# Two-layer MLP behind retention and a Fourier mix: the half-sums of weights and tokens at other program steps

## The chip, the cores and the metric

One core of one Trainium2 chip runs the whole kernel in one launch. The metric is the device time of one execution in microseconds, the median over runs. TensorE is PE in the profile, VectorE DVE, ScalarE ACT, GpSimd POOL, SyncE SP.

## The reference

Everything is float32, with B=2, S=768 tokens, 512 features, and a hidden width of 2048. The MLP weights come as float64.

```python
def _moe_ref(x, w_ch1, w_ch2):            # x: the retention layer's output
    X = np.fft.fft(np.fft.fft(x, axis=1), axis=2)
    u = x + np.real(X)
    un = (u - mean(u)) / np.sqrt(var(u) + 1e-06)
    return u + np.maximum(un @ w_ch1, 0.0) @ w_ch2

def _moe2_ref(x, g_ln, w_ch1, w_ch2):
    xn = (x - mean(x)) / np.sqrt(var(x) + 1e-06) * g_ln
    return x + np.maximum(xn @ w_ch1, 0.0) @ w_ch2
```

Ahead of them stands a retention layer (block-wise attention with decay, 8 heads of 64).

## The kernel before, in words

Every float32 operand of a matmul is split into a high and a low float16 half, and three products (high-high, high-low, low-high) are added up. The program runs batch 0's retention and Fourier mix in an order written out by hand, and then a main loop (L1020) over program steps n = 0 to 127 and three more. Step n stands for layer m = n // 64, token block blk (16 steps each; a block is 384 tokens, two for each batch) and hidden tile f = n % 16. Steps 0 to 63 are layer one (m = 0), steps 32 to 47 its block 2, the first block of batch 1.

At a step stand, in this order: the up-projection of the step's tile (`mlp_up`, L655, with its matmuls in L662, or `mlp_up_fast`, L733, matmuls in L752), the background tasks that `put` (L939) entered for the step, and the down-projection `mlp_down` of the tile three steps back (matmuls in L799). Batch 1's retention and Fourier mix, the normalisation of later blocks and the conversion of weights are such background tasks. A scheduler places the instructions of each engine from this program order; each engine runs its own in that order, so a late instruction holds all behind it on the same engine.

The plain up-projection of a tile is 12 matmuls of 384 columns. The fast one computes two tiles together by a seven-product scheme (as Strassen's), on 192 columns. Its operands are sums of quarters: for the weights, `w1_sums(m, g, kk)` (L682) for group g of four tiles (f = 4g to 4g+3) and half kk of the features; for the tokens, `un_sums(m, blk, kk)` (L710). One call of `w1_sums`, a **unit** in the text below, issues on DVE two sums of a high and a low half (L695) and four sums of quarters (L700 to L703), then two casts on ACT (L706) and two subtractions on POOL (L707). One call of `un_sums` issues two L715 and L720 to L723 on DVE, two casts on ACT (L727) and two subtractions on POOL (L728). The first product of a pair needs no sum; the second needs both halves kk of weights and tokens.

In layer one the fast form is used from tile 4 of block 2 on (`F02` = 4, in `fast_from`, L1006): groups 1, 2 and 3 are first used at steps 36, 40 and 44, group 0 at step 48, in block 3. The sums of block 1's tokens are made and not used.

Each plain tile leaves PE through one `mlp_act` (L674): ACT writes the high half (L676), DVE the low half (L677), and only then is its PSUM bank, one of two in the pool "up", free for the tile two steps on. In the fast form ACT copies the first product (L764), DVE adds (L765, L772, L773, L778, L779), and PE writes over the same banks in between, so that PE waits for L765 and L772 within a pair; ACT and DVE take the result out in L784 and L785.

The steps of the units before: group 2 at 15 and 16, group 3 at 19 and 20, group 0 at 28 and 29, group 1 at 32 and 33. Block 1's token sums stand at 17 and 18, block 2's at 34 and 35. The normalisation of block 2 (three tiles of 128 tokens, `ln_a`, `ln_n`, `ln_b`) stands at the end of the Fourier mix of batch 1, just ahead of step 32, and its last act is a pair of transposing transfers on SP (L627) into `unT`, from which block 2's first matmul reads.

Where the sums lie: `i` in L684 numbers the units, and picks a room for each: two tiles of the loading pool "ld" (i < 3), the rooms of the mask and of three tables that are no longer needed (i = 3 to 6), or the two state tiles (i = 7).

Of the kernel before, what the change touches and what calls it, by code (L numbers as in the profile page):

```python
# [49 lines left out]
ONPOOL = "Y1 Y2 o0 o1 k0 k1 k2 j0 j1 j2"  # L50
LD1 = ()
LD2 = ()
EARLY0, GATEN, B1, SPC, DS, DC, DFO, DD, D1S, D2S, AO, YA, NR, NE, LN1, L1, L2, F01, F02, S2, S0, SD, TL, R1, R2, SE, PR0, PR1, LAG, UB, FB, NW, MQ, SPL = 11, 8, 3, 2.0, 2.0, 5, 1.0, 0.5, 0.5, 1.0, "aba", "aa", 2, 0, 2, 2.5, 2.5, 16, 4, 15, 28, 1, 3, 1.5, 2, "dddd_dppp", 0, 0, 3, 3, 13, 11, 1, 3

KEEP = -(1 << 30)
REST = (1 << 30) - 1
# [57 lines left out]
def tile_retention_fourier_mlp(ctx: ExitStack, tc: tile.TileContext, a: dict, out: bass.AP):  # L114
# [23 lines left out]
    def f32t(name, spare=None):  # L138
        if spare is not None:
            return wpool.tile([P, 512], F32, tag=f"w2_{spare}", name=name)  # L140
        return fp.tile([P, 512], F32, tag="f", name=name)

    def hl(name):
        return fp.tile([P, 2, 512], F16, tag="f", name=name)
# [536 lines left out]

    def w1_sums(m, g, kk, r=None):  # L682
        w = w1t[m, g]
        i = (2 * g + kk - 4) % 8  # L684
        if 3 <= i < 7:
            t = const.tile([P, 2, 2, 2, 256], F16, tag=f"big{i - 3}", name=f"sw{m}_{g}_{kk}")
            t = [t[:, 0], t[:, 1]]
        elif i < 3:
            t = [ldp.tile([P, 2, 2, 256], F16, tag="ld", name=f"sw{m}_{g}_{kk}_{x}") for x in range(2)]
        else:  # L690
            t = [const.tile([P, 2, 2, 256], F16, tag=f"state{x}", name=f"sw{m}_{g}_{kk}_{x}") for x in range(2)]
        if r is None:
            r = [f32t(f"wr{m}_{g}_{k}") for k in (kk, kk + 2)]
            for x, k in enumerate((kk, kk + 2)):
                dve.tensor_tensor(r[x], w[:, 0, k], w[:, 1, k], op=ALU.add)  # L695
        eng = [pool if z == "p" else dve for z in SE.split("_")[m]]
        (a11, a21), (a12, a22) = ([z.rearrange("p (q a f) -> p q a f", a=2, f=P)[:, :, x] for x in range(2)] for z in r)
        s12, s34 = (f32t(f"ws{x}_{m}_{g}_{kk}") for x in (12, 34))
        s1, s2, s3, s4 = (z[:, x * 256:x * 256 + 256].rearrange("p (q f) -> p q f", f=P) for z in (s12, s34) for x in range(2))
        eng[0].tensor_tensor(s1, a21, a22, op=ALU.add)  # L700
        eng[1].tensor_tensor(s2, s1, a11, op=ALU.subtract)
        eng[2].tensor_tensor(s3, a11, a21, op=ALU.subtract)
        eng[3].tensor_tensor(s4, a12, s2, op=ALU.subtract)  # L703
        for x, z in enumerate((s12, s34)):
            hi, lo = (t[x][:, y].rearrange("p s f -> p (s f)") for y in range(2))
            act.copy(hi, z)  # L706
            pool.tensor_tensor(lo, z, hi, op=ALU.subtract)  # L707
        sw[m, g, kk] = t

    def un_sums(m, blk, kk):  # L710
        x = unT[m, blk]
        r = []
        for k in (kk, kk + 2):
            t = f32t(f"tr{m}_{blk}_{k}")[:, :TB]
            dve.tensor_tensor(t, x[:, 0, k], x[:, 1, k], op=ALU.add)  # L715
            r += [t[:, :HB], t[:, HB:]]
        b11, b12, b21, b22 = r
        t12, t34 = (f32t(f"ts{y}_{m}_{blk}_{kk}")[:, :TB] for y in (12, 34))
        t1, t2, t3, t4 = t12[:, :HB], t12[:, HB:], t34[:, :HB], t34[:, HB:]
        dve.tensor_tensor(t1, b12, b11, op=ALU.subtract)  # L720
        dve.tensor_tensor(t2, b22, t1, op=ALU.subtract)
        dve.tensor_tensor(t3, b22, b12, op=ALU.subtract)
        dve.tensor_tensor(t4, b21, t2, op=ALU.subtract)  # L723
        tw[m, blk, kk] = []
        for y, z in enumerate((t12, t34)):
            t = hl(f"th{y}_{m}_{blk}_{kk}")[:, :, :TB]
            act.copy(t[:, 0], z)  # L727
            pool.tensor_tensor(t[:, 1], z, t[:, 0], op=ALU.subtract)  # L728
            tw[m, blk, kk].append(t)
# [209 lines left out]
    def put(n, task):  # L939
        bg.setdefault(max(int(n), 0), []).append((n, len(bg), task))  # L940

    def later(task, offset):
        def run():
            with tc.high_priority(offset=-offset):
                task()
        return run
# [14 lines left out]
    n = t + DC + DFO  # L961
# [28 lines left out]
    def w1_unit(p):  # L990
        g, kk, half = p // 4, p % 4 // 2, p % 2
        t = w_conv(1, 1, 4 * g + kk + 2 * half)
        if not half:
            first[g, kk] = t
        else:
            w1_sums(1, g, kk, (first.pop((g, kk)), t))
# [5 lines left out]
    def step(n):  # L1002
        m = n // (NB * NF)
        return m, order[m][n // NF % NB], n % NF
# [3 lines left out]
    for (m, blk), f in fast_from.items():  # L1008
        for kk in range(2):
            if m == 0 and blk < 3:  # L1010
                put(16 * blk + f / 2 + kk - (7 if blk == 1 else 0), lambda blk=blk, kk=kk: un_sums(0, blk, kk))
            else:
                at = m * NB * NF + order[m].index(blk) * NF
                put(at - TL + 2 * kk, lambda m=m, blk=blk, kk=kk: un_sums(m, blk, kk))
    for g in range(4):
        for kk in range(2):
            n = (S2 if g > 1 else S0) + 4 * (g % 2) + SD * kk
            put(n, later(lambda g=g, kk=kk: w1_sums(0, g, kk), PR0))

    for n in range(total + LAG):  # L1020
        rest = None
        if n < total:
            m, blk, f = step(n)
# [34 lines left out]
```

## Time and profile before

| what | value |
|---|---|
| time, median of 3 runs | 645.83 us (644.15 to 646.98) |
| the profiled execution's own time | 646.34 us |
| its span, first to last instruction | 644.5 us |
| mean granted clock of TensorE | 0.968 of 2.4 GHz |
| PE busy | 587.3 us, 91% |
| DVE busy | 470.2 us, 73% |
| POOL busy | 296.0 us, 46% |
| ACT busy | 259.4 us, 40% |

Times in the views are microseconds from the start of the span, the mean of one instruction in nanoseconds. "xN" counts instructions, and a bracket at a row's end gives the idle time of the engine just ahead of it and what ended it. Matmuls are pipelined, so the duration of a row of N matmuls is less than N times that of one.

### The profile page before, as it was taken

The page shows a single profiled execution, that of the slowest core. Times are in us where ns is not written, and L with a number is a line of the kernel's source. Part 1 is how long each engine was busy: PE and PEld are TensorE (multiplying, and loading weights), DVE is VectorE, ACT ScalarE, POOL GpSimd, SP SyncE. Part 2 cuts the span into 40 slices and gives each one's busy share as a digit, 9 for nine tenths or more (in the row PEclk, how much of TensorE's full clock was granted, in tenths as well). Part 3 has the DMA queues.
Part 4 walks back from the last instruction along what each step waited for, and adds up shares of the span by engine and source line. Part 5 has one row for each costly group of instructions (what it writes and reads, how often), then busy time and mean ns, then how long its engine had stood idle before and what let it go on. Part 6 is the DMA issues. An engine that isn't in the chain of part 4 may idle for free.

```text
span 644.5 us, 11965 instructions
## 1 busy us (share of the span) xinstructions
PE 587.3 (91%) x4704; PEld 384.2 (60%) x4704; DVE 470.2 (73%) x985; ACT 259.4 (40%) x524; POOL 296.0 (46%) x303
## 2 busy tenths in 40 slices
PE   6868878979998999859999988799999999999997
PEld 4743734545554454437676755576677676777773
DVE  5999798998599945965569999999663653454333
ACT  3634557764433332233226754575323222321111
POOL 6865767876536456372116886598211210120000
PEclk8879988999999999989999998999999999999999
DMA  8971017975200001001115664384020015201001
GB/s 286 395 295 48 20 67 194 258 245 177 91 1 1 1 9 33 9 16 26 10 34 146 181 147 129 102 204 108 1 67 17 17 54 55 41 2 70 30 1 50
DMA packets 44020, 58.66 MB, mean 91 GB/s; under 512 B 25919, under 2 KB 27836, under 8 KB 43964
## 3 DMA queue, kind: packets, MB, share of 16 engines
q1 hardware_dynamic: 43292, 57.82, 30.9%
q8 instruction: 37, 0.61, 0.4%
q10 hardware_dynamic: 672, 0.08, 0.1%
q14 instruction: 19, 0.16, 0.1%
HBM read 49.23 MB, written 4.72 MB: 84 GB/s over the span
## 4 chain that ended last, share of the span: by engine, by line
PE 59%; DVE 27%; issue 5%; POOL 4%; ACT 3%; DMA 2%; DVEq 0%; ACTq 0%; SPq 0%; POOLq 0%
PE ps_y L799 28%; PE ps L752 21%; PE ps_h L662 4%; DVE wf L259 3%; DVE ps_w L255 3%; DVE ps_w L257 2%; DVE bst L596 2%; DMA ws<-in_w 2%; DVE tr L715 1%; POOL m L320 1%; DVE h L677 1%; PE ps_s L308 1%; PE ps_d L484 1%; DVE wr L695 1%; POOL w L272 1%
## 5 line engine op out<-in xcount | busy, mean ns | idle before, releaser
L799 PE MATMUL ps_y<-w,h 128*128 128x512 f16 x1152 | 280.5, 381 | 4.6 <-ACT h L784 2.2
L799 PEld LDWEIGHTS <-h 128*128 128x128 f16 x1152 | 109.6, 98 | 108.3 <-ACT h L784 5.0
L752 PEld LDWEIGHTS <-sw 128*128 128x128 f16 x1104 | 96.9, 100 | 25.9 <-issue 11.7
L752 PE MATMUL ps<-th,sw 128*128 128x192 f16 x828 | 94.8, 252 | 9.5 <-ACT th L727 7.4
L272 POOL TENSOR_TENSOR w<-wf,w 128x512 f16<-128x512 f32 x64 | 75.3, 1182 | 53.9 <-ACT w L270 53.7
L752 PEld LDWEIGHTS <-w 128*128 128x128 f16 x828 | 72.0, 98 | 22.5 <-issue 6.3
L662 PE MATMUL ps_h<-unT,w 128*128 128x384 f16 x396 | 75.9, 335 | 9.2 <-DVE h L677 5.1
L784 ACT ACTIVATE h<-ps 128x384 f16<-128x384 f32 x92 | 43.4, 488 | 68.4 <-DVE ps L778 58.6
L752 PE MATMUL ps<-unT,w 128*128 128x192 f16 x552 | 62.5, 247 | 3.1 <-DVE h L677 3.1
L662 PEld LDWEIGHTS <-w 128*128 128x128 f16 x396 | 38.1, 100 | 41.2 <-issue 10.6
L728 POOL TENSOR_TENSOR th<-ts,th 128x384 f16<-128x384 f32 x28 | 25.4, 924 | 65.2 <-ACT th L727 65.1
L772 DVE TENSOR_TENSOR t<-ps,s 128x192 f32<-128x192 f32 x46 | 16.3, 354 | 53.3 <-PE ps L752 53.3
L785 DVE SCALAR_TENSOR_TENSOR h<-ps,h 128x384 f16<-128x384 f32 x92 | 48.8, 552 | 5.8 <-ACT h L784 4.5
L707 POOL TENSOR_TENSOR sw<-ws,sw 128x512 f16<-128x512 f32 x32 | 40.4, 1276 | 21.5 <-ACT sw L706 21.5
L764 ACT COPY s<-ps 128x192 f32<-128x192 f32 x46 | 14.6, 317 | 82.4 <-PE ps L752 82.3
L269 ACT ACTIVATE wf<-wf 128x512 f32<-128x512 f32 x48 | 30.1, 629 | 37.2 <-DVE wf L259 37.1
L625 POOL TENSOR_TENSOR uns<-un,uns 128x512 f16<-128x512 f32 x21 | 25.1, 1195 | 41.7 <-ACT uns L624 41.7
L255 DVE TENSOR_SCALAR ps_w<-ws 128x512 int32<-128x512 int32 x54 | 37.0, 687 | 3.7 <-DMA ws<-in_w 3.0
L270 ACT CAST w<-wf 128x512 f16<-128x512 f32 x64 | 39.2, 615 | 1.2
L765 DVE TENSOR_TENSOR s<-ps,s 128x192 f32<-128x192 f32 x46 | 16.2, 352 | 30.6 <-ACT s L764 30.6
L604 POOL TENSOR_TENSOR rs<-rs,neghalf 128x1 f32<-128x1 f32 x24 | 13.6, 573 | 53.3 <-DVE rs L602 52.9
L259 DVE SCALAR_TENSOR_TENSOR wf<-ws,ps_w 128x512 int32<-128x512 int32 x54 | 36.6, 678 | 1.1
(153 smaller groups left out, 880.9 us busy)
## 6 DMA issues: line engine op xcount, KB each, us to landing
ws<-in_w SPq DMA_DIRECT2D x25, 512.0 KB, 4.7
ws<-in_w2b SPq DMA_DIRECT2D x16, 512.0 KB, 3.3
ws<-in_w1b SPq DMA_DIRECT2D x16, 512.0 KB, 4.0
kt<-in_kt SPq DMA_DIRECT2D x12, 256.0 KB, 5.4
qt<-in_qt SPq DMA_DIRECT2D x12, 256.0 KB, 5.4
v<-in_v SPq DMA_DIRECT2D x12, 256.0 KB
k<-in_k SPq DMA_DIRECT2D x12, 256.0 KB, 3.3
pre<-in_w SPq DMA_DIRECT2D x4, 512.0 KB, 6.6
```

The lines of the kernel that those rows point to most:

```text
L255: dve.tensor_scalar(part, raw[:, :, 1], 3, REST, op0=ALU.logical_shift_left, op1=ALU.bitwise_and)
L259: dve.scalar_tensor_tensor(ti, raw[:, :, 0], 29, part, op0=ALU.logical_shift_right, op1=ALU.bitwise_or)
L269: act.activation(t, t, AF.Copy, scale=sc)
L270: act.copy(hi, t)
L272: (dve if m == 0 and i in (LD1 if kind == 1 else LD2) else pool).tensor_tensor(lo, t, hi, op=ALU.subtract)
L662: pe.matmul(ps, w[:, i, k, fo:fo + P], x[:, j, k, :], start=n == 0, stop=n == 11)
L707: pool.tensor_tensor(lo, z, hi, op=ALU.subtract)
L728: pool.tensor_tensor(t[:, 1], z, t[:, 0], op=ALU.subtract)
L752: pe.matmul(ps, lhs, rhs, start=start and n == 0, stop=n == 5, skip_group_check=True)
L784: act.activation(hi, z, AF.Relu)
L785: dve.scalar_tensor_tensor(lo, z, 0.0, hi, op0=ALU.max, op1=ALU.subtract)
L799: pe.matmul(dn[blk][j], h[:, x, j * P:(j + 1) * P], w[:, y], start=f == 0 and n == 0, stop=f == NF - 1 and n == 2)
```

## The change

The units of layer one get a table of steps, in the order in which the groups are used: group 1 at 16 and 18, group 2 at 20 and 25, group 3 at 28 and 30, group 0 at 36 and 40. Block 2's token sums go from steps 34 and 35 to 31 and 32; block 1's stay. The number i of a unit's room becomes 2g + kk - 2 modulo 8, so that the first three units in the new order take the "ld" tiles; this holds for layer two as well, whose units stay at their steps. `later(..., PR0)` with PR0 = 0 falls away.

```diff
-EARLY0, GATEN, ... F01, F02, S2, S0, SD, TL, R1, R2, SE, PR0, PR1, LAG, ... = 11, 8, ... 16, 4, 15, 28, 1, 3, 1.5, 2, "dddd_dppp", 0, 0, 3, ...
+EARLY0, GATEN, ... F01, F02, TL, R1, R2, SE, PR1, LAG, ... = 11, 8, ... 16, 4, 3, 1.5, 2, "dddd_dppp", 0, 3, ...
+
+SUMS = {(1, 0): 16, (1, 1): 18, (2, 0): 20, (2, 1): 25, (3, 0): 28, (3, 1): 30, (0, 0): 36, (0, 1): 40}
...
-        i = (2 * g + kk - 4) % 8
+        i = (2 * g + kk - 2) % 8
...
-                put(16 * blk + f / 2 + kk - (7 if blk == 1 else 0), lambda blk=blk, kk=kk: un_sums(0, blk, kk))
+                put(16 * blk + f / 2 + kk - (7, 3)[blk - 1], lambda blk=blk, kk=kk: un_sums(0, blk, kk))
...
-    for g in range(4):
-        for kk in range(2):
-            n = (S2 if g > 1 else S0) + 4 * (g % 2) + SD * kk
-            put(n, later(lambda g=g, kk=kk: w1_sums(0, g, kk), PR0))
+    for (g, kk), n in SUMS.items():
+        put(n, lambda g=g, kk=kk: w1_sums(0, g, kk))
```

No instruction is added or taken away on any engine (PE 8906 rows, DVE 974, ACT 523, POOL 305, SP 161 in both). From line 56 to the last edit the changed file's line numbers are two higher. In the rows below, `wr_g_k` and `ws_0_g_kk` are the weight sums of group g, `sw_g_kk` their halves, `tr`, `ts` and `th` the same for tokens, `h_b_p` pair p of hidden tiles of block b, `ps_h_b_f` the up-projection of tile f, and `u`, `un`, `uns` the normalisation.

**Place 1: the end of block 1, ACT.** First before, then with the change: `h_1_7<-ps_h_1_15` is the last hidden tile of block 1, `un_2_2` the last tile of tokens of block 2's normalisation.

```order
L534 ACTIVATE qs_189<-ps_pq_2_3037 128x128
L534 ACTIVATE qs_189<-ps_pq_2_3037 128x127
L676 ACTIVATE h_1_7_3254<-ps_h_1_14_3241 128x384
L676 ACTIVATE h_1_7_3254<-ps_h_1_15_3266 128x384
L616 ACTIVATE un_2_2_3089<-u_120,rs_2_2_3062 128x512
L624 CAST uns_2_2_3092<-un_2_2_3089 128x512
L571 ACTIVATE cosy_2_3099<-ps_pq_2_3037 128x129
```

```order
L536 ACTIVATE qs_189<-ps_pq_2_3022 128x128
L536 ACTIVATE qs_189<-ps_pq_2_3022 128x127
L678 ACTIVATE h_1_7_3239<-ps_h_1_14_3226 128x384
L708 CAST sw_2_1_3074<-ws_0_2_1_3079 128x512
L708 CAST sw_2_1_3074<-ws_0_2_1_3080 128x512
L678 ACTIVATE h_1_7_3239<-ps_h_1_15_3266 128x384
L618 ACTIVATE un_2_2_3089<-u_120,rs_2_2_3047 128x512
L626 CAST uns_2_2_3092<-un_2_2_3089 128x512
L573 ACTIVATE cosy_2_3099<-ps_pq_2_3022 128x129
```

The two casts of group 2's second unit now stand ahead of the last hidden tile. On DVE the unit's six sums stand in the same place, around `u<-u,qs` and ahead of `u<-ps_pq_2`, on which the normalisation goes on; before and with the change:

```order
L615 SCALAR_TENSOR_TENSOR rs_2_1_2994<-mv_2_1_2992,rs_2_1_2994 128x1
L539 TENSOR_TENSOR u_120<-u_120,qs_189 128x257
L677 SCALAR_TENSOR_TENSOR h_1_7_3254<-ps_h_1_14_3241,h_1_7_3254 128x384
L677 SCALAR_TENSOR_TENSOR h_1_7_3254<-ps_h_1_15_3266,h_1_7_3254 128x384
L549 SCALAR_TENSOR_TENSOR u_120<-ps_pq_2_3037,u_120 128x256 x2
```

```order
L617 SCALAR_TENSOR_TENSOR rs_2_1_2979<-mv_2_1_2977,rs_2_1_2979 128x1
L697 TENSOR_TENSOR wr_2_1_3075<-w_0_2_1396 128x512
L697 TENSOR_TENSOR wr_2_3_3076<-w_0_2_1396 128x512
L541 TENSOR_TENSOR u_120<-u_120,qs_189 128x257
L702 TENSOR_TENSOR ws_0_2_1_3079<-wr_2_1_3075,wr_2_3_3076 128x256
L704 TENSOR_TENSOR ws_0_2_1_3080<-wr_2_1_3075 128x256
L679 SCALAR_TENSOR_TENSOR h_1_7_3239<-ps_h_1_14_3226,h_1_7_3239 128x384
L703 TENSOR_TENSOR ws_0_2_1_3079<-ws_0_2_1_3079,wr_2_1_3075 128x256
L705 TENSOR_TENSOR ws_0_2_1_3080<-wr_2_3_3076,ws_0_2_1_3079 128x256
L679 SCALAR_TENSOR_TENSOR h_1_7_3239<-ps_h_1_15_3266,h_1_7_3239 128x384
L551 SCALAR_TENSOR_TENSOR u_120<-ps_pq_2_3022,u_120 128x256 x2
```

Two sums went ahead of the row with `qs`, four behind it, on both sides of the hidden tile `h_1_7<-ps_h_1_14`.

**Place 2: the first steps of block 2, DVE**, up to the release of the banks of hidden tiles 2 and 3 (`h_2_1`); before and with the change:

```order
L702 TENSOR_TENSOR ws_0_1_1_3352<-wr_1_1_3347 128x256
L715 TENSOR_TENSOR tr_2_0_3393<-unT_2_2945 128x384
L715 TENSOR_TENSOR tr_2_2_3395<-unT_2_2945 128x384
L615 SCALAR_TENSOR_TENSOR rs_3_2_3665<-mv_3_2_3663,rs_3_2_3665 128x1
L677 SCALAR_TENSOR_TENSOR h_2_1_3383<-ps_h_2_2_3370,h_2_1_3383 128x384
L703 TENSOR_TENSOR ws_0_1_0_3312<-wr_1_2_3308,ws_0_1_0_3311 128x256
L701 TENSOR_TENSOR ws_0_1_1_3351<-ws_0_1_1_3351,wr_1_1_3347 128x256
L720 TENSOR_TENSOR ts_0_2_0_3397<-tr_2_0_3393 128x192
L722 TENSOR_TENSOR ts_0_2_0_3398<-tr_2_2_3395,tr_2_0_3393 128x192
L599 BN_AGGR mv_0_2_4531<-bst_0_2_4529 128x2
L703 TENSOR_TENSOR ws_0_1_1_3352<-wr_1_3_3348,ws_0_1_1_3351 128x256
L677 SCALAR_TENSOR_TENSOR h_2_1_3383<-ps_h_2_3_3421,h_2_1_3383 128x384
```

```order
L705 TENSOR_TENSOR ws_0_3_1_3248<-wr_3_3_3244,ws_0_3_1_3247 128x256
L723 TENSOR_TENSOR ts_0_2_0_3285<-tr_2_2_3283,ts_0_2_0_3285 128x192
L617 SCALAR_TENSOR_TENSOR rs_3_2_3649<-mv_3_2_3647,rs_3_2_3649 128x1
L679 SCALAR_TENSOR_TENSOR h_2_1_3384<-ps_h_2_2_3371,h_2_1_3384 128x384
L725 TENSOR_TENSOR ts_0_2_0_3286<-tr_2_2_3283,ts_0_2_0_3285 128x192
L601 BN_AGGR mv_0_2_4532<-bst_0_2_4530 128x2
L717 TENSOR_TENSOR tr_2_1_3322<-unT_2_2930 128x384
L717 TENSOR_TENSOR tr_2_3_3324<-unT_2_2930 128x384
L598 BN_STATS bst_1_2_5473<-u_119 128x6
L722 TENSOR_TENSOR ts_0_2_1_3326<-tr_2_1_3322 128x192
L724 TENSOR_TENSOR ts_0_2_1_3327<-tr_2_3_3324,tr_2_1_3322 128x192
L679 SCALAR_TENSOR_TENSOR h_2_1_3384<-ps_h_2_3_3406,h_2_1_3384 128x384
```

Four weight sums (`ws`) in these rows have become one, and the second half of the token sums (`tr_2_1`, `tr_2_3`) is begun ahead of tile 3's row rather than behind it.

**Place 3: the first fast pair of block 2, DVE** (`s_2_4`, `t_2_5`); before and with the change:

```order
L615 SCALAR_TENSOR_TENSOR rs_0_0_4181<-mv_0_0_4179,rs_0_0_4181 128x1
L599 BN_AGGR mv_1_0_5121<-bst_1_0_5119 128x2
L765 TENSOR_TENSOR s_2_4_3473<-ps_2_4_3474,s_2_4_3473 128x192
L772 TENSOR_TENSOR t_2_5_3517<-ps_2_4_3474,s_2_4_3473 128x192
L765 TENSOR_TENSOR s_2_6_3555<-ps_2_6_3556,s_2_6_3555 128x192
L773 TENSOR_TENSOR ps_2_4_3475<-ps_2_4_3475,t_2_5_3517 128x192
L602 TENSOR_SCALAR rs_0_1_4339<-mv_0_1_4337 128x1
L778 TENSOR_TENSOR ps_2_4_3474<-ps_2_4_3474,s_2_4_3473 128x192
```

```order
L601 BN_AGGR mv_1_0_5123<-bst_1_0_5121 128x2
L697 TENSOR_TENSOR wr_0_0_3466<-w_0_0_742 128x512
L697 TENSOR_TENSOR wr_0_2_3467<-w_0_0_742 128x512
L767 TENSOR_TENSOR s_2_4_3442<-ps_2_4_3443,s_2_4_3442 128x192
L702 TENSOR_TENSOR ws_0_0_0_3470<-wr_0_0_3466,wr_0_2_3467 128x256
L704 TENSOR_TENSOR ws_0_0_0_3471<-wr_0_0_3466 128x256
L703 TENSOR_TENSOR ws_0_0_0_3470<-ws_0_0_0_3470,wr_0_0_3466 128x256
L705 TENSOR_TENSOR ws_0_0_0_3471<-wr_0_2_3467,ws_0_0_0_3470 128x256
L774 TENSOR_TENSOR t_2_5_3501<-ps_2_4_3443,s_2_4_3442 128x192
L775 TENSOR_TENSOR ps_2_4_3444<-ps_2_4_3444,t_2_5_3501 128x192
L767 TENSOR_TENSOR s_2_6_3539<-ps_2_6_3540,s_2_6_3539 128x192
L780 TENSOR_TENSOR ps_2_4_3443<-ps_2_4_3443,s_2_4_3442 128x192
```

Group 0's first unit now stands around the row of `s_2_4`, four of its sums ahead of `t_2_5`; its second unit stands in the same way around `s_2_8`.

## Rows read from the trace of the kernel before

**Rows 1.** Busy time of each engine by stretch (core 0), then granted clock and DMA.
```profile
254.00:286.00 32.00, 20.97 (x116) 10.73 (x114) 30.17 (x60) 10.47 (x22) 19.10 (x17) 0.97 0.07 13
286.00:310.00 24.00, 23.25 (x183) 17.70 (x183) 11.57 (x31) 7.24 (x16) 5.13 (x6) 0.89 0.19 29
```
**Rows 2.** Waits of PE from 195 to 310 us: total, times, longest.
```profile
PE ps L752 <- ACT th L727: 4.9, 1, 4.9
PE ps L752 <- DVE h L677: 3.1, 2, 2.1
PE ps_h L662 <- DVE h L677: 2.6, 1, 2.6
PE ps_d L484 <- ACT fhl L474: 2.3, 2, 1.7
PE ps L752 <- DVE t L772: 0.4, 1, 0.4
PE ps_h L662 <- DMA unT<-uns: 0.4, 1, 0.4
PE ps L752 <- DVE s L765: 0.2, 1, 0.2
```
**Rows 3.** PE in order of time, 245 to 296 us: start, duration, instruction.
```profile
249.31 7.72 PE L799 MATMUL ps_y<-w,h 128*128 128x512 f16 x35
...
286.08 4.16 PE L752 MATMUL ps<-th,sw 128*128 128x192 f16 x25 [4.95 <-ACT th L727]
290.40 1.00 PE L752 MATMUL ps<-th,sw 128*128 128x192 f16 x6 [0.16 <-DVE s L765]
...
292.84 0.66 PE L752 MATMUL ps<-th,sw 128*128 128x192 f16 x6
293.33 0.66 PE L752 MATMUL ps<-unT,w 128*128 128x192 f16 x6
```
**Rows 4.** Busy time by stretch, as Rows 1, five microseconds.
```profile
285.00:290.00 5.00, 3.92 (x25) 3.72 (x25) 1.11 (x6) 1.32 (x4) 1.79 (x3) 0.50 0.15 30
```
**Rows 5.** DVE by line, 254 to 286 us: count, busy us, mean ns.
```profile
L695 DVE TENSOR_TENSOR wr<-w 128x512 f32<-128x512 f16 x8 | 6.6, 866 | 0.0
...
L703 DVE TENSOR_TENSOR ws<-wr,ws 128x256 f32<-128x256 f32 x4 | 3.1, 771 | 0.0
L701 DVE TENSOR_TENSOR ws<-ws,wr 128x256 f32<-128x256 f32 x4 | 2.3, 581 | 0.0
L702 DVE TENSOR_TENSOR ws<-wr 128x256 f32<-128x256 f32 x4 | 2.2, 544 | 0.0
...
L715 DVE TENSOR_TENSOR tr<-unT 128x384 f32<-128x384 f16 x4 | 2.1, 568 | 0.0
...
L700 DVE TENSOR_TENSOR ws<-wr,wr 128x256 f32<-128x256 f32 x4 | 1.8, 441 | 0.0
```
**Rows 6.** DVE in order of time, 179 to 256 us.
```profile
180.01 2.88 DVE L695 TENSOR_TENSOR wr<-w 128x512 f32<-128x512 f16 x2
...
245.43 0.80 DVE L539 TENSOR_TENSOR u<-u,qs 128x257 f32<-128x257 f32 x1 [2.22 <-ACT qs L534]
...
249.16 0.56 DVE L677 SCALAR_TENSOR_TENSOR h<-ps_h,h 128x384 f16<-128x384 f32 x1 [2.47 <-ACT h L676]
...
254.34 1.28 DVE L695 TENSOR_TENSOR wr<-w 128x512 f32<-128x512 f16 x2
```
**Rows 7.** ACT in order of time, 247 to 275 us.
```profile
248.63 0.49 ACT L676 ACTIVATE h<-ps_h 128x384 f16<-128x384 f32 x1 [2.87 <-PE ps_h L662]
...
272.25 1.14 ACT L706 CAST sw<-ws 128x512 f16<-128x512 f32 x2 [3.98 <-DVE ws L703]
```
**Rows 8.** POOL in order of time, 179 to 283 us.
```profile
179.63 2.72 POOL L320 TENSOR_TENSOR m<-m,m 128x512 f16<-128x512 f32 x2 [2.55 <-ACT m L318]
...
248.82 0.72 POOL L560 TENSOR_TENSOR u<-u,qs 128x255 f32<-128x255 f32 x1
...
280.95 1.89 POOL L728 TENSOR_TENSOR th<-ts,th 128x384 f16<-128x384 f32 x2
```

More of the change, by code (lines that the diff above doesn't have):

```diff
@@ L52 @@
 LD2 = ()
-EARLY0, GATEN, B1, SPC, DS, DC, DFO, DD, D1S, D2S, AO, YA, NR, NE, LN1, L1, L2, F01, F02, S2, S0, SD, TL, R1, R2, SE, PR0, PR1, LAG, UB, FB, NW, MQ, SPL = 11, 8, 3, 2.0, 2.0, 5, 1.0, 0.5, 0.5, 1.0, "aba", "aa", 2, 0, 2, 2.5, 2.5, 16, 4, 15, 28, 1, 3, 1.5, 2, "dddd_dppp", 0, 0, 3, 3, 13, 11, 1, 3
+EARLY0, GATEN, B1, SPC, DS, DC, DFO, DD, D1S, D2S, AO, YA, NR, NE, LN1, L1, L2, F01, F02, TL, R1, R2, SE, PR1, LAG, UB, FB, NW, MQ, SPL = 11, 8, 3, 2.0, 2.0, 5, 1.0, 0.5, 0.5, 1.0, "aba", "aa", 2, 0, 2, 2.5, 2.5, 16, 4, 3, 1.5, 2, "dddd_dppp", 0, 3, 3, 13, 11, 1, 3
+SUMS = {(1, 0): 16, (1, 1): 18, (2, 0): 20, (2, 1): 25, (3, 0): 28, (3, 1): 30, (0, 0): 36, (0, 1): 40}
 KEEP = -(1 << 30)
```

## The prediction

> **What bounds the kernel now.** I first look at busy time by stretch [rows 1]. From 254 to 286 us PE is busy 20.97 of 32 us, DVE 30.17: here DVE sets the pace and PE waits. In the next 24 us it is the other way round: PE 23.25, DVE 11.57. The reader is to see that a full engine in one stretch has room in the next, so that work moved from one stretch to the other can pay.
>
> Next the waits of PE [rows 2]. They are the loss that the page's busy shares hide: 4.9 us for a token half on ACT (L727), 3.1 and 2.6 us for banks that DVE's row L677 frees, 2.3 us for the folded tokens of the Fourier mix (L474), 0.4 us for the transposes ahead of block 2, 0.6 us for L772 and L765 in the first fast pairs. Then the rows in time [rows 3]: behind the longest wait, 25 matmuls took 4.16 us, and six more 1.00 us, where six take 0.66 us later. The granted clock says why: 0.50 from 285 to 290 us [rows 4], which is the lower of TensorE's two levels, 1.2 of 2.4 GHz. The clock fell in the 4.95 us in which PE stood still; the waits of 2.6 and 2.1 us just before had left it alone.
>
> Who fills DVE from 254 to 286 us? The lines of the units [rows 5]: L695 6.6, L703 3.1, L701 2.3, L702 2.2, L700 1.8 us, 16.0 us for four units, 4.0 each. These are the units of groups 0 and 1, of which group 0 is not read before block 3.
>
> **The change part by part.** Work is neither added nor taken away, so everything is order. I sum against the profiled execution, 646.34 us, which is 0.51 us above the median of 645.83.
>
> *Two units leave the full stretch.* Group 3's two units stand in it instead of four of groups 0 and 1, 8.0 us less work on DVE. In place 2 of the order, DVE reaches the row that frees tile 2's bank with one weight sum on the way instead of several, and the token sums, now at steps 31 and 32, are begun ahead of tile 3's row. So DVE is ahead of PE at both banks: the 3.1 us go. The second half of the token sums is then done about when PE has run the first products and the down-projections ahead of them, where it came 4.9 us late: that goes too. -8.0 us, which is the best end; the other is 0, if DVE is no earlier for all that. I take the best end since 8.0 us less work stand against waits of 8.0 us in one queue. Late next is POOL, whose two low halves of that sum take 1.89 us [rows 8]; the first is needed two products in. I take +0.5, between 0 and 1.9.
>
> *The clock.* With no wait of 4.95 us the clock should stay up. Twenty-five matmuls at 0.082 us (293.33 less 292.84, by six [rows 3]) and a last one's 0.25 take 2.2 us in place of 4.16, and six 0.66 in place of 1.00: -2.3 us. Bounds 0 and -2.3.
>
> *The wait for tile 0's bank, 2.6 us,* stays: ahead of that row DVE's list is as long as before, with two L715 (568 ns each) in place of two L695 (866 ns) [rows 5]. -0.6, bounds -1.2 and 0.
>
> *The second unit of group 2, place 1.* It now stands in the chain that ends in block 2's first matmul. Before, DVE had 2.22 us idle ahead of L539 and 2.47 us ahead of the last hidden tile [rows 6], 4.7 us for a unit of 4.0; if it fitted, it would cost nothing. It does not fit well, since its four quarter sums stand behind L539, the two casts behind those, and ACT's last hidden tile behind the casts. From L539's end at 246.2: four sums 9.4/4 = 2.35 and a hidden tile 0.5 make 249.1; the second cast ends some 0.6 later [rows 7], ACT's tile 0.49 and DVE's 0.56 later still, 250.8 in place of 249.7. With hand-overs between engines the normalisation goes on some 1.2 later, and PE, which has 35 down-projections (7.72 us) as cover [rows 3] and used them up 0.4 us too soon already, waits that much more. I take +1.2. If the whole unit lay on the chain it would be +4.0; if the gaps took it, 0.
>
> That price rests on a slow DVE. The same pair of L695 takes 1.28 us at 254.34 and 2.88 us at 180.01 [rows 6], where POOL ran L320 through it, from 179.63 for 2.72 us; and at the new place POOL ends a row that had no idle time ahead of it only at 249.5 [rows 8]. The Trainium skill (GPSIMD Engine Reference, Key points) says that GpSimd shares its SBUF interfaces with VectorE and contends with instructions of two SBUF inputs. By that rule this place speaks against the change, and the trace agrees (2.88 against 1.28). Without the rule the pair fits in the first gap and the term is nearer 0, and the sum 1.2 lower.
>
> *The fold before.* On POOL the add that begins the third fold now stands behind both pairs of token subtractions of block 1 instead of one, some 1.9 us each [rows 8], and DVE's fold has one more hidden tile in it, 0.5. That is up to 2.4 later; PE comes 0.8 later itself, since three down-projections (0.22 each) and a plain matmul (0.16) went ahead. DVE had gaps on the way, so I take half of the first: 2.3 becomes 2.7, +0.4, bounds -2.3 and +2.4.
>
> *Group 0's units in the fast steps, place 3.* DVE has room there (11.57 of 24 us), but the order within a pair counts. Two L695 stand ahead of s_2_4, 1.7 us, four sums ahead of t_2_5, 2.35 us; PE has other products for about 1.3 us at either. A net wait of 1.3 per unit makes 2.6, in place of the 0.6 there now: +2.0. Bounds -0.6 and +8.0, two units in full.
>
> *At nothing:* the new rooms. Layer two keeps its own order, and each room's last reader is done steps before; if one were not, the cover is the whole of a block's step and PE would wait for a cast. Block 2's later stretch is full PE in any case, so what is gained before 310 us should reach the end.
>
> Sum: -8.0 + 0.5 - 2.3 - 0.6 + 1.2 + 0.4 + 2.0 = -6.8, 639.5 us in the profiled execution, 639.0 as a median.
>
> **The rivals.** *The stall only moves (no change).* The chain of place 1 takes the whole unit, +4.0, and the fast steps +5.0, half way to their bound. Then -6.8 + 2.8 + 3.0 = -1.0, 644.8 us. For it: DVE's list is not shorter, and the two places where units went both lie near PE's need. Against: DVE's 11.57 of 24 us and the 4.7 us of gaps. 0.20.
>
> *All is covered.* Place 1 fits into its gaps (0) and the fast steps cost what they do now (0): -6.8 - 1.2 - 2.0 = -10.0, 635.8 us. Against it is the order: sums stand ahead of rows that PE waits for. 0.13.
>
> *Slower: the fast pairs take over the long wait.* Each of group 0's units holds t_2_5, or the same row two tiles on, for its whole 4.0 us and some, PE stands still for about as long as the 4.95 us that brought the clock down, and pays 2.3 us at the low level, twice. Then the term is 12.6 in place of 2.0: -6.8 + 10.6 = +3.8, 649.6 us. It decides when such a wait nears 5 us; below 2.6 us the clock has not been seen to fall. For it: DVE keeps strict order. Against: POOL is nearly idle there, and PE has down-projections between. 0.07.
>
> *The change does not do what it says* is ruled out as far as the order goes, which shows the rows moved, so it has no chance of its own.
>
> **How the numbers follow.** Forecast 0.60, no change 0.20, all covered 0.13, slower 0.07. A measurement of this kernel can tell about 0.5%, 3.2 us: below 642.6 is faster, above 649.1 slower. The forecast's own spread, from the bounds of single terms, is about 636 to 643, of which a little (0.04) lies above 642.6. So faster 0.60 - 0.04 + 0.13 = 0.69, within 0.5% 0.04 + 0.20 = 0.24, slower 0.07. The range 635.0 to 645.5 holds the forecast, most of the covered case and over half of the no-change one; both signs are not in it.
>
> **What would show it.** In the changed profile (lines two higher): the 4.9 us wait for the token half and the 3.1 us for banks gone from PE's waits in the first ten steps of block 2; granted clock 1.00 through the first fast pair; DVE's weight-sum lines at half their count between block 2's first matmul and the fast pair; the wait for the transposes at 1.5 to 2 us in place of 0.4; waits for the rows L767 and L774 (now L765, L772) summing to 2 or 3 us, none near 5. I am wrong if the token half is late again (then DVE was not what made it late), if the wait for the transposes is 4 us or more (first rival), or if a fast pair halves the clock (slower).

## The result, and the profile after

The changed kernel takes **636.88 us** (median of 4 runs, 635.34 to 639.0) beside 646.4 us (4 runs, 644.15 to 647.6) for the kernel before: a ratio of 0.986 with the interval 0.981 to 0.990. Forecast were 639.0 us and a range of 635.0 to 645.5. The profiled execution took 638.23 us (span 636.4), 8.1 less than before's 646.34; forecast were 6.8 less.

Waits of PE in the changed kernel, 195 to 310 us (its lines stand two higher than before's):

```profile
PE ps_h L664 <- DMA unT<-uns: 2.0, 1, 2.0
PE ps L754 <- DVE s L767: 1.7, 1, 1.7
PE ps_h L664 <- DVE h L679: 1.0, 2, 0.7
PE ps_d L486 <- ACT fhl L476: 0.8, 1, 0.8
PE ps L754 <- DVE t L774: 0.6, 1, 0.6
PE ps_y L801 <- ACT h L786: 0.2, 1, 0.2
```

Against [rows 2], the 4.9 us for the token half and the 3.1 us for the fast pair's banks are gone. The transposes' wait has grown from 0.4 to 2.0 us, those of the first fast pair from 0.6 to 2.5. PE in order of time, same kernel:

```profile
258.85 5.74 PE L664 MATMUL ps_h<-unT,w 128*128 128x384 f16 x24 [1.98 <-DMA unT<-uns]
...
266.74 2.11 PE L664 MATMUL ps_h<-unT,w 128*128 128x384 f16 x12 [0.75 <-DVE h L679]
...
277.65 1.88 PE L754 MATMUL ps<-th,sw 128*128 128x192 f16 x20
...
282.48 0.66 PE L754 MATMUL ps<-th,sw 128*128 128x192 f16 x6 [1.67 <-DVE s L767]
...
284.21 0.66 PE L754 MATMUL ps<-th,w 128*128 128x192 f16 x6 [0.58 <-DVE t L774]
```

The products that stood 4.95 us and then ran at the low clock [rows 3] run on without a wait: 20 in 1.88 us. Not forecast is the first row: 24 matmuls in 5.74 us where before the same 24 took 4.06. Busy time by stretch, as [rows 1]:

```profile
254.00:286.00 32.00, 27.02 (x173) 16.06 (x172) 27.84 (x65) 12.07 (x24) 17.97 (x19) 0.95 0.09 18
286.00:310.00 24.00, 23.79 (x193) 16.44 (x191) 14.58 (x38) 6.88 (x16) 6.03 (x7) 1.00 0.12 23
```

DVE is off its ceiling in the first stretch, and PE is busy six microseconds longer there, 1.7 of which are the slow 24 matmuls.

**Two fixed points.** Spans hide part of the effect, since executions differ before anything was moved. I take two rows of DVE: A, the last hidden tile's row ahead of the first moved unit, and B, the last s row of the program. Up to A, DVE's list is the same in both kernels and in every run below. DVE in order of time, the kernel before, then the changed kernel:

```profile
176.88 0.56 DVE L677 SCALAR_TENSOR_TENSOR h<-ps_h,h 128x384 f16<-128x384 f32 x1 [2.70 <-ACT h L676]
...
241.03 0.56 DVE L677 SCALAR_TENSOR_TENSOR h<-ps_h,h 128x384 f16<-128x384 f32 x1
...
627.72 0.36 DVE L765 TENSOR_TENSOR s<-ps,s 128x192 f32<-128x192 f32 x1 [2.53 <-ACT s L764]
```

```profile
178.11 0.56 DVE L679 SCALAR_TENSOR_TENSOR h<-ps_h,h 128x384 f16<-128x384 f32 x1 [2.70 <-ACT h L678]
...
240.88 0.56 DVE L679 SCALAR_TENSOR_TENSOR h<-ps_h,h 128x384 f16<-128x384 f32 x1
...
619.63 0.36 DVE L767 TENSOR_TENSOR s<-ps,s 128x192 f32<-128x192 f32 x1 [2.52 <-ACT s L766]
```

From A to B the kernel before takes 450.84 us, the changed one 441.52: 9.3 less. The changed kernel's profile was 1.2 us late at A by chance, which is why its span shows 8.1 only.

### The profile page after: what moved, and what is told of

The parts are those of the page before. It is cut to its first block, busy times and chain, and to the rows that moved or that the text cites. A ratio compares the mean times of both kernels' runs of the same rounds, so it can differ in the third digit from the quotient of the medians.

```text
span 636.4 us, 11966 instructions
## 1 busy us (share of the span) xinstructions
PE 587.2 (92%) x4704; PEld 384.3 (60%) x4704; DVE 465.5 (73%) x985; ACT 259.4 (41%) x524; POOL 295.4 (46%) x303
## 4 chain that ended last, share of the span: by engine, by line
PE 59%; DVE 25%; issue 5%; POOL 4%; ACT 3%; DMA 3%; SPq 0%; DVEq 0%; POOLq 0%; ACTq 0%
PE ps_y L801 28%; PE ps L754 21%; PE ps_h L664 4%; DVE wf L261 3%; DVE ps_w L257 2%; DMA ws<-in_w 2%; DVE ps_w L259 2%; DVE bst L598 2%; PE ps_d L486 1%; DVE tr L717 1%; PE ps_s L310 1%; PE ps_o L390 1%; DVE h L679 1%; DVE vhl L291 1%; DVE wr L697 1%
## 5 line engine op out<-in xcount | busy, mean ns | idle before, releaser
L754 PEld LDWEIGHTS <-sw 128*128 128x128 f16 x1104 | 95.1, 98 | 22.6 <-issue 7.8
L754 PE MATMUL ps<-th,sw 128*128 128x192 f16 x828 | 93.0, 247 | 6.1 <-DVE s L767 3.6
L664 PE MATMUL ps_h<-unT,w 128*128 128x384 f16 x396 | 78.7, 343 | 8.6 <-DVE h L679 4.6
L709 POOL TENSOR_TENSOR sw<-ws,sw 128x512 f16<-128x512 f32 x32 | 38.6, 1218 | 24.5 <-ACT sw L708 24.5
L259 DVE SCALAR_TENSOR_TENSOR ps_w<-ws,ps_w 128x512 int32<-128x512 int32 x54 | 36.7, 685 | 0.4
```

The costliest lines, as they stand in the source:

```text
L259: dve.scalar_tensor_tensor(part, raw[:, :, 1], KEEP, part, op0=ALU.bitwise_and, op1=ALU.bitwise_or)
L664: pe.matmul(ps, w[:, i, k, fo:fo + P], x[:, j, k, :], start=n == 0, stop=n == 11)
L754: pe.matmul(ps, lhs, rhs, start=start and n == 0, stop=n == 5, skip_group_check=True)
```

## The experiments

All are compared by median with the kernel before, which ran beside each of the three groups of runs (645.3, 645.4 and 645.0 us), and by A to B, which is one execution each. Lines in them are those of the kernel before.

| run | median us | ratio, 95% interval | A to B us |
|---|---|---|---|
| changed kernel again | 637.34 | 0.983 to 0.989 | 441.42 |
| token sums alone | 643.81 | 0.996 to 0.999 | 449.68 |
| units alone | 640.02 | 0.990 to 0.995 | 446.46 |
| group 0 later | 638.36 | 0.986 to 0.991 | 445.18 |
| units alone, late order kept | 635.29 | 0.981 to 0.988 | 440.67 |
| group 2 early | 634.47 | 0.979 to 0.986 | 441.52 |
| no unread sums | 632.61 | 0.976 to 0.983 | 438.53 |
| group 0 later, late order kept | 636.11 | 0.981 to 0.988 | 443.06 |
| group 0 alone moved | 635.60 | 0.982 to 0.990 | 441.61 |
| best parts | 631.23 | 0.975 to 0.983 | 437.47 |
| old rooms | 636.24 | 0.983 to 0.989 | 441.47 |

### Which part of the change pays

**The changed kernel again**, nothing edited.

> The changed kernel once more, nothing edited, to see what in its profile recurs. Its first profile (638.23 us) was 1.2 us behind the kernel before from 147 us on, in steps that nothing had moved, and ran 24 matmuls in 5.74 us instead of 4.06 behind the transposes' wait of 1.98 us. Theory: both belong to that execution, 1.2 and 1.7 us, and the two quicker executions of that set, 635.3 and 635.5, are those without them. Then this profile lies within 1 us of 638.2 less what of the two is absent: 635.3 with neither, 636.5 to 637 with one. Rival: the fallen clock is fixed by the order, since PE always stands for 2 us there. Then the 24 matmuls take over 5 us here too. Place 1's wait of 1.5 to 2 us is expected in either case, and a median of 636 to 638 us.

PE in order of time:

```profile
257.23 4.06 PE L662 MATMUL ps_h<-unT,w 128*128 128x384 f16 x24 [1.97 <-DMA unT<-uns]
...
265.11 2.11 PE L662 MATMUL ps_h<-unT,w 128*128 128x384 f16 x12 [2.34 <-DVE h L677]
...
280.85 0.66 PE L752 MATMUL ps<-th,sw 128*128 128x192 f16 x6 [1.67 <-DVE s L765]
```

The same wait of 1.97 us, and the 24 matmuls take 4.06 again: the order alone does not make the clock fall. The fall was also free, against what I expected: this execution took 636.53 us, which is 638.23 less the 1.6 us by which A stands sooner, and not the 635.3 of the theory. With the slow 24, tile 0's bank is waited for 0.75 us; without, 2.34. DVE sets the pace there, so the next row begins 7.9 us after the 24 either way (266.74 less 258.85, 265.11 less 257.23). A to B agrees to 0.1 us.

**Token sums alone**, on the kernel before:

```diff
-                put(16 * blk + f / 2 + kk - (7 if blk == 1 else 0), ...
+                put(16 * blk + f / 2 + kk - (7, 3)[blk - 1], ...
```

> The kernel before with only block two's token sums moved (steps 31 and 32), all weight units where they were. Theory (DVE's list is as long as before in 254 to 286 us, so four units still stand ahead of the first fast pair): the wait of 4.9 us moves from the token half to the sums of group 1's unit, which now stand behind the token sums; time 643 to 648 us, 0.4% or less from the kernel before. Rival (the token sums only stood too late): the 4.9 us wait and the 2.3 us of halved clock go without the weight units being touched; 638 to 641 us.

643.81 us, as the theory has it. The long waits only changed their names; the two longest waits of PE, 195 to 310 us:

```profile
PE ps L752 <- ACT sw L706: 4.4, 1, 4.4
PE ps L752 <- POOL sw L707: 2.7, 1, 2.7
```

**Units alone**: the changed kernel with the token sums back at 34 and 35.

```diff
-                put(16 * blk + f / 2 + kk - (7, 3)[blk - 1], ...
+                put(16 * blk + f / 2 + kk - (7, 0)[blk - 1], ...
```

> The changed kernel with the token sums put back to steps 34 and 35, so that only the weight units stand in the new order. Theory (8 us less work on DVE in that stretch is what pays): most of the gain stays, 637 to 640 us, with a wait for the token half of 0 to 2 us and the bank waits of the kernel before, 3.1 us, gone. Rival (the token sums' place is what pays): the token half is still 3 us or more late, and the clock halves; 641 to 645 us.

At 640.02 us, the edge of what the theory gave, it is 5.3 faster than the kernel before, and the token half is not late. Waits of PE, 195 to 310 us:

```profile
PE ps_h L662 <- DMA unT<-uns: 2.0, 1, 2.0
PE ps L752 <- DVE t L772: 1.1, 2, 0.7
PE ps_h L662 <- DVE h L677: 0.9, 2, 0.7
PE ps_d L484 <- ACT fhl L474: 0.8, 1, 0.8
PE ps L752 <- POOL th L728: 0.5, 1, 0.5
```

So the theory holds for block 2, and the 4.9 us came from the units, not from the token sums' step. But in the end the run is 2.7 us slower than the changed kernel, and it loses that behind 340 us. PE's waits from 345 to 470 us sum to 14 us instead of 10; the two largest have grown from 1.6 and 0.8 us:

```profile
PE ps_y L799 <- ACT h L784: 4.9, 8, 2.3
PE ps L752 <- DVE t L772: 3.1, 6, 0.7
```

The scheduler had laid out DVE's list anew there: only its last 200 rows stand as before, against 524 in the changed kernel.

**Units alone, late order kept**: in SUMS, one step, by which the last 515 rows stand as before.

```diff
-(0, 1): 40
+(0, 1): 41
```

> The run with the units alone (token sums at 34 and 35) with one unit, the second of group 0, a step later (41). With that, DVE's last 515 rows, from the second fast pair of block 2 on, stand in the same order as in the kernel before and in the changed kernel; in the run with the units alone only the last 200 did, and behind 340 us PE waited 14 us there where the changed kernel waits 10. Theory (that run was ahead of the changed kernel by 2.5 us at block two's end and lost it to the other order behind 340 us): the lead is kept, PE's waits from 345 to 470 us sum to 10 us as in the kernel before, 634 to 636 us. Rival (whoever comes to DVE's full stretch from 340 us on earlier waits longer there, in any order): 638 to 641 us.

635.29 us, with waits of 9.8 us from 345 to 470, the same lines and amounts as in the kernel before. One step of one unit is worth 4.7 us (5.8 from A to B), through an order far behind it. The theory holds; the rival is out. Within this order the token sums' new place brings nothing (440.67 without it, 441.42 with it).

**Group 0 alone moved**, one edit on the kernel before:

```diff
-            n = (S2 if g > 1 else S0) + 4 * (g % 2) + SD * kk
+            n = (S2 if g > 1 else S0) + 4 * (g % 2) + SD * kk if g else 36 + 5 * kk
```

> The kernel before with one edit: group 0's two units at 36 and 41 in place of 28 and 29. Groups 1, 2 and 3, both token sums and the rooms stay as they were; DVE's last 515 rows keep their order. Theory (two units, 8 us of DVE, in the stretch ahead of block two's first fast pair are the whole cause): waits of 4.9 and 3.1 us gone, the transposes' wait still 0.4 us, the folded tokens' wait still 2.3 us as in the kernel before, and 634.5 to 637 us, the changed kernel's time or better. Rival (the order of use matters too: group 1's units, not yet done, take over the wait, as with the token sums moved alone): PE waits 2 us or more for L706, L707 or L727 ahead of the first fast pair, 638.5 to 642 us.

```profile
PE ps_h L662 <- DVE h L677: 2.3, 1, 2.3
PE ps_d L484 <- ACT fhl L474: 2.3, 2, 1.7
PE ps L752 <- DVE t L772: 1.1, 2, 0.7
PE ps L752 <- POOL th L728: 0.5, 1, 0.5
PE ps_h L662 <- DMA unT<-uns: 0.4, 1, 0.4
```

635.60 us, and 441.61 from A to B: all of the change's gain from one line. Both long waits are gone, with 1.0 us more of short ones (L772, L728) in the first fast pairs, and the fold's and the transposes' waits are those of before. The new order of the other groups adds nothing on the whole: what the changed kernel gains at the fold (1.4 us) it pays again at place 1 (1.5).

**Old rooms**, on the changed kernel:

```diff
-        i = (2 * g + kk - 2) % 8
+        i = (2 * g + kk - 4) % 8
```

> The changed kernel with the rooms of the kernel before, (2g + kk - 4) % 8. Theory (a room's last reader is done steps before the next unit writes it): the same waits and 635.5 to 638.5 us, within 0.3% of the changed kernel. Rival (some room now holds a unit back): a cast of the units, L706 or L707, starts later and PE waits for it, 639 us or more.

636.24 us and 441.47: the rooms cost and bring nothing. (The transposes were waited for 2.5 us and tile 0's bank 0.4, in an execution whose clock fell between them.)

### The prices that the change pays

**Group 0 later**, in SUMS of the changed kernel:

```diff
-(0, 0): 36, (0, 1): 40
+(0, 0): 40, (0, 1): 44
```

> The changed kernel with group 0's two units four steps later (40 and 44 in place of 36 and 40), out of the first fast pair. Theory (the two L695 ahead of s_2_4 and the four sums ahead of t_2_5 make the waits of 1.67 and 0.58 us): both waits go back to 0.2 and 0.4 us as in the kernel before, and a pair two steps on has 1 us or less in their place; 1 to 2 us faster than the changed kernel, 634.9 to 636 us. Rival (s_2_4 is late because DVE's row of L604 ahead of it waits 1.3 us for ACT and the next for POOL, which no unit causes): a wait of 1 us or more for L767 stays at the first pair, and the time is within 0.5 us of the changed kernel's.

The waits for L765 (1.67) and the second 0.2 are gone, that for L772 is 0.4, as the theory has it; yet the run is not faster, 638.36 us. In this execution the clock fell earlier, behind tile 0's bank, where PE had no slack left:

```profile
255.16 4.06 PE L662 MATMUL ps_h<-unT,w 128*128 128x384 f16 x24 [1.98 <-DMA unT<-uns]
...
263.04 3.47 PE L662 MATMUL ps_h<-unT,w 128*128 128x384 f16 x12 [2.34 <-DVE h L677]
```

So PE reaches hidden tile 3 1.7 us later from A than in the changed kernel, and that alone would have hidden most of the wait for L765. DVE's row of `s_2_4` itself stands 1.2 us sooner from A (102.77 against 103.97 us).

And DVE's list behind 340 us was another, with 289 rows at the end unchanged. PE's waits from 345 to 470 us sum to 10 us there as in the changed kernel, but from 380 to 405 us the granted clock is 0.81, 0.51, 1.00, 0.67 and 0.98 in windows of five microseconds, where the changed kernel has 0.66 in one of them; 3.1 us of the 3.7 lost from A to B are lost behind 340 us. Whether the other order brings the clock down there or chance did is open. So I repeated it with 400: **group 0 later, late order kept**.

```diff
-(0, 0): 36, (0, 1): 40
+(0, 0): 40, (0, 1): 45
```

> The changed kernel with group 0's units at 40 and 45 (40 and 44 in the run before that moved them), by which DVE's last 400 rows stay in the order of the changed kernel (289 there). Theory (moving the units out of the first pair saved 2.0 us up to 330 us, and the order behind 340 us gave it back): 634.5 to 636.5 us, 1 to 2.5 us faster than the changed kernel. Rival (group 0's units cost as much wherever they stand, since DVE is full from 340 us on and they now stand nearer to it): 637 to 639 us.

636.11 us, inside the theory's range, but too near the changed kernel's to tell the two expectations apart; A to B says 1.6 slower, in an execution whose clock fell behind tile 0's bank as in the run before. Waits of PE, 300 to 345 us, where the changed kernel has none:

```profile
PE ps_y L799 <- ACT h L784: 1.4, 1, 1.4
PE ps L752 <- ACT th L727: 0.3, 1, 0.3
```

The units' price moved with them: 1.7 us here, for at most 2.0 saved at the first pair. That is the rival's mechanism; my theory stands only for the first pair, and there only in part, since PE came later here too.

**Group 2 early**, in SUMS of the changed kernel:

```diff
-(2, 1): 25
+(2, 1): 22
```

> The changed kernel with the second unit of group 2 at step 22 in place of 25, out of the chain that ends in block two's first matmul; the last 614 rows of DVE in the same order as in the changed kernel. Theory (the unit put 1.5 us on that chain): the wait for the transposes goes back from 2.0 to about 0.4 us and the row that frees tile 0's bank comes as much sooner, so 635 to 636.5 us, 1 to 2 us faster than the changed kernel. Rival (the unit only moves its 4 us ahead of the folded tokens' rows L496, which PE's transforms wait for): the transposes' wait is gone and PE waits 1.5 us or more longer in 215 to 250 us; 637 to 640 us.

634.47 us, half a microsecond below the theory's range. The transposes' wait falls to 0.5 us, the fold's stays at 0.8 (the rival is out), and up to 345 us the run is 1.4 ahead. Its A to B is nonetheless the changed kernel's, since the clock took the 1.4 back in layer two. There PE waits 1.72 us for L727 in both; windows of five microseconds behind it, first the changed kernel again, then this run:

```profile
380.00:385.00 5.00, 2.27 (x20) 1.91 (x19) 5.00 (x12) 2.14 (x5) 2.68 (x4) 0.85 0.21 63
385.00:390.00 5.00, 5.00 (x31) 3.05 (x30) 4.51 (x10) 2.15 (x5) 3.14 (x3) 0.80 0.43 150
```

```profile
380.00:385.00 5.00, 5.00 (x26) 3.78 (x26) 4.23 (x9) 3.11 (x7) 3.86 (x4) 0.50 0.60 198
385.00:390.00 5.00, 5.00 (x33) 2.96 (x32) 3.80 (x8) 1.56 (x3) 1.26 (x2) 0.91 0.28 79
```

The median, over executions with either luck, shows the gain: 2.9 us less than the changed kernel, if with intervals that overlap.

### A version that beats both

**No unread sums**: units alone, late order kept, and block 1's token sums left out. Left out are sums that no product reads.

```diff
-        for kk in range(2):
+        for kk in range(2 * (blk != 1 or m)):
```

> The run before the last (units alone, late order kept) without the token sums of block one, which no product reads: 12 rows of DVE, 4 of ACT and 4 of POOL less around 180 to 200 us. DVE's last 515 rows in the same order. Theory (the wait for the folded tokens, 0.8 us, and the normalisation behind it are paced by DVE, so that 12 rows, some 4.7 us by their rows, pull the fold forward): the 0.8 us goes and the normalisation comes up to 1 us sooner; 0.5 to 2 us faster than that run. Rival (POOL or PE paces the fold; PE is busy all of 150 to 200 us): within 0.5 us of that run.

632.61 us, 2.7 less than that run, and 2.1 from A to B, somewhat more than the theory's 0.5 to 2. Neither the folded tokens nor the transposes are waited for; a wait of 1.9 us for a hidden tile on ACT (L676) is new:

```profile
PE ps_h L662 <- DVE h L677: 2.0, 1, 2.0
PE ps_y L799 <- ACT h L676: 1.9, 1, 1.9
PE ps L752 <- DVE t L772: 0.4, 1, 0.4
```

**Best parts**: this, with two steps in SUMS.

```diff
-(2, 1): 25, (0, 1): 41
+(2, 1): 22, (0, 1): 40
```

> What helped, together: the changed kernel's steps with the second unit of group 2 at 22, the token sums at 34 and 35, and without block one's token sums that nothing reads; DVE's last 554 rows in the same order. Theory (each term is a piece of DVE's list ahead of a row that PE waits for, so they add where DVE still sets the pace): against the run without block one's sums, DVE has 1.4 us less ahead of tile 0's bank, whose wait falls from 2.0 to about 0.6 us; 630.5 to 632.5 us. Rival (with the fold and the transposes no longer waited for, PE itself is the pace there): the same 632 to 633.5 us as that run.

**631.23 us**, 2.1% less than the kernel before (interval 1.7 to 2.5) and the best of the study. From A to B it is 1.1 ahead of the last run; their intervals overlap. The time is the theory's, but the wait is not: tile 0's did not fall to 0.6. The 2.0 us there and the 1.9 ahead of it became 1.3 and 1.3, with DVE rows of the residual (L807) and the normalisation (L602) named in place of a hidden tile's.

```profile
PE ps_h L662 <- DVE rs L602: 1.3, 1, 1.3
PE ps_y L799 <- DVE u L807: 1.3, 1, 1.3
PE ps L752 <- DVE t L772: 0.5, 1, 0.5
```

## Why the prediction was right, and where it was not

| step of the prediction | forecast | measured |
|---|---|---|
| two units leave the full stretch | -8.0 | -8.05: the waits of 4.95, 2.15 and 0.95 us are gone |
| POOL's low halves late next | +0.5 | 0 (0.5 only with the token sums at 34 and 35) |
| the clock at the first fast pair | -2.3 | -2.3: 0.082 us a product again |
| tile 0's bank | -0.6 | -0.27 (2.61 to 2.34, in the changed kernel's second profile) |
| place 1, group 2's second unit | +1.2 | +1.54 (transposes 0.44 to 1.98) |
| the fold | +0.4 | -1.4 |
| group 0's units in the fast steps | +2.0 | +1.85 (0.61 to 2.46) |

The measured terms sum to -8.6 of the 9.3 to 9.4 from A to B; the last 0.7 stands in no single wait. **The main term is shown, and sharper than forecast**: one edit, group 0's two units, gives the whole gain. The prediction credited the token sums' earlier step with part of it; that is refuted by the two runs that left them at 34 and 35. A unit holds ACT and POOL too, and no run separates the three engines. That DVE was the one that made PE wait is read from its busy 30.17 of 32 us [rows 1] and, in the kernel before, from the idle time of the very cast that PE waited 4.95 us for:

```profile
285.52 0.96 ACT L727 CAST th<-ts 128x384 f16<-128x384 f32 x2 [2.30 <-DVE ts L721]
```

**The fold is the step that failed**, by its sign: "+0.4, bounds -2.3 and +2.4". I looked at POOL, put the fold up to 2.4 us later there and took half. From A to the hidden tile's row at 241.03 and 240.88 DVE takes 64.15 us before and 62.77 after. ACT's casts of the three folds (L474) begin 30.62, 35.57 and 39.45 us behind A before, and 30.86, 35.10 and 38.38 us with the change: the first 0.2 later, the third 1.1 sooner. POOL's add for the third does end 0.9 later from A, at 212.77 us, but DVE takes it up only at 213.04, behind its own rows. PE comes the 0.8 later that the prediction counted, so its transforms wait 0.8 us for the folds instead of 2.3 and end 1.2 nearer to A.

The run that moved group 0 alone, whose other units stand where they stood, has the 2.3 us again. The number of units is not the cause: in both kernels DVE has two between A and the third fold's last row, and the run with group 2 early, whose fourth unit stands ahead of the transforms' rows as in the kernel before, waits 0.8 us all the same. What differs is what these two cost: their pairs of L695 took 2.88 and 2.95 us before, 1.28 and 1.29 with the change. That this brought the third fold forward is likely, and no run shows it. The bounds did hold the term.

**Place 1 had the right size for partly the wrong reason.** I rested its price on a slow pair of L695, 2.88 us with POOL at work [rows 6, 8], and took 2.35 us for the four quarter sums. The pair was quick, and the sums took 3.18. DVE in order of time in the changed kernel, one of group 1's sums first, then place 1:

```profile
186.42 0.41 DVE L702 TENSOR_TENSOR ws<-wr,wr 128x256 f32<-128x256 f32 x1
...
242.91 1.28 DVE L697 TENSOR_TENSOR wr<-w 128x512 f32<-128x512 f16 x2
245.21 0.80 DVE L541 TENSOR_TENSOR u<-u,qs 128x257 f32<-128x257 f32 x1 [1.02 <-ACT qs L536]
245.93 0.94 DVE L702 TENSOR_TENSOR ws<-wr,wr 128x256 f32<-128x256 f32 x1
246.80 0.94 DVE L704 TENSOR_TENSOR ws<-wr 128x256 f32<-128x256 f32 x1
...
248.13 0.47 DVE L703 TENSOR_TENSOR ws<-ws,wr 128x256 f32<-128x256 f32 x1
248.64 0.83 DVE L705 TENSOR_TENSOR ws<-wr,ws 128x256 f32<-128x256 f32 x1
250.55 0.56 DVE L679 SCALAR_TENSOR_TENSOR h<-ps_h,h 128x384 f16<-128x384 f32 x1 [1.08 <-ACT h L678]
```

The pair ran in a gap, ahead of L541. The sums behind it paid: 0.83 to 0.94 us for three of the four, where such a row takes 0.41 at 186.42, when POOL stood idle; from 245.7 to 250 us POOL ran adds without a pause (0.90 us each). The Trainium skill (GPSIMD Engine Reference, Key points) says that GpSimd shares its SBUF interfaces with VectorE and contends with instructions of two SBUF inputs; by that rule, these are the rows to suffer, and the trace agrees in three of four (the fourth took 0.47). That this unit was the price is shown by the run that moved it to 22: 2.0 back to 0.5 us.

**The fast steps** cost what was forecast by luck. The prediction gave each of group 0's units a wait of 1.3 us; the first pair has the whole 2.5 us, and around `s_2_8`, where the second unit stands, PE waits for nothing. Nor is it the unit alone: DVE's rows ahead of the first pair waited 1.34 us for ACT and 1.07 for POOL (L604 and L617 at 278.44 and 279.67) before the unit began. With the units moved four steps on, these two waits stand as they were (1.34 and 1.06) and the row of `s_2_4` comes 1.2 us sooner from A, so that of the 1.67 us some 1.2 are the unit's, an estimate from one execution each.

**The clock.** The prediction held that below a wait of 2.6 us it had not been seen to fall; it can, behind 1.98 us here (24 matmuls in 5.74 us). Through the first fast pair the granted clock is 1.00, as forecast. No rival came in: no wait of the fast pairs is near 5 us, the transposes' wait is far from 4, and the gain is there. The forecast is some 2 us too high, most of it the fold, which gained 1.4 where +0.4 was forecast.

## What to carry to other kernels

When one engine is full ahead of a stage and PE waits, ask of each piece of work in its list when its result is first read; the one not read until a stage later is the one to move, and here that single move was the whole gain. After each move, compare the order of the whole list, not only the place edited: a scheduler can lay out a later stage anew, and a neighbouring step that keeps the old order there was worth 4.7 us. To judge a microsecond, measure from a point ahead of the first moved instruction.

## What was not expected of the hardware

The same order, at the same wait, does not always bring the clock down. Behind a wait of 1.97 or 1.98 us at the transposes the 24 matmuls took 5.74 us in one execution of the changed kernel and 4.06 in another; behind 2.34 us at tile 0's bank the next twelve took 3.3 to 3.5 us in two runs and 2.11 in five others. In layer two, around a wait of 1.72 us, the granted clock is below 1.00 for a different time in different executions, which shifted one run by 1.4 us. At the transposes, where another engine sets the pace, the fallen clock cost nothing.

Executions also differ before anything differs in their lists: A stood between 172.40 and 178.11 us in the thirteen profiles of this study. That alone is 5.7 us, nearly as much as the spread between the runs of one kernel (the kernel before in the first group: 640.9 to 647.7 us).
